# Weight pairs of a three-layer kernel: stored as pairs, and their low parts moved off GpSimd

## The chip, the cores and the metric

The kernel runs on one core of a Trainium2 chip. The time is that of the whole program on the device, in microseconds (us). TensorE (PE in the rows) multiplies matrices, VectorE (DVE) and ScalarE (ACT) do the elementwise work, GpSimd (POOL) can do some of it too, and SyncE (SP) issues most of the DMA transfers; GpSimd issues some from a queue of its own.

## What is computed

Three layers, each on the output of the one before it, all in float32:

```python
scores = where(causal, -1e9, q @ k.T / 8)                 # B, H, S, D = 4, 8, 576, 64
local  = softmax(scores) @ v
mem    = (phi(q) @ M_prev) / (phi(q) @ z_prev + 1e-6)     # phi(x) = elu(x) + 1
x      = g * mem + (1 - g) * local                        # g = sigmoid(beta); 2304 tokens x 512
h = x @ moe_w_in;   x = (s * relu(h)**2 + b) @ moe_w_out  # first layer: 512 -> 2048 -> 512
h = x @ moe2_w_in;  x = (h * tanh(softplus(h))) @ moe2_w_out   # second layer, same sizes
```

## The kernel before

**Pairs.** TensorE takes its operands in a format shorter than float32 (`F32R`). Each float32 operand is therefore held as a pair: the high part is a cast by ScalarE, the low part is the difference between the operand and its high part. A product is then three matmuls: high by high, high by low, low by high. The function `split` (L710) makes a pair; its argument `lo_on` says which engine makes the difference, and the helper line L717 records all of these differences, on either engine. L716 is the cast.

**First layer.** Its weights stay in SBUF as pairs (`wih`, `wil` for w_in, `woh`, `wol` for w_out, in four quarters `r`). The first 1536 tokens go through them in plain products (L823 and L902): four blocks of 256 tokens and one of 512.

**Block stages.** The last 768 tokens of the first layer are block 0, and the second layer is blocks 1 to 3 of 768 tokens. These use a scheme with seven products in place of eight (Winograd's form of Strassen): the operands are quarters of the matrices and sums of them. For the weights these are three quarters as they are and four sums: in w_in A00, A01, A11 and S0 to S3, in w_out B00, B10, B11 and T1 to T4. Each block has a hidden stage, eight steps `q` of seven products (L1040; the elementwise work of a step is in `hidden`, L1024), and an output stage, seven products `p` over all eight `q` (L1117, in block 0 L1120; evacuations L1108 to L1155 are in `out_product` and `out_block`).

**Where block weights come from.** For layer 1, `resident` (L773) puts the parts together again on GpSimd (L780), forms the sums, and stores all seven slots as float32 in DRAM (L790, arrays `WID[1]`, `WOD[1]`). For layer 2, `convert` (L665) turns the raw input words into float32, and `combine_in` and `combine_out` (L735, L754) form the sums on VectorE (L731) and store seven slots (L725, `WID[2]`, `WOD[2]`). `load_wi` and `load_wo` (L998, L1015) load slots back as float32 into staging tiles (`wf`, in the stage area) and split them into tiles of the ring `W`, which has four places; a hidden step and an output product each use two. GpSimd makes the differences for both w_in and w_out in block 0 and for w_out in every later block; VectorE makes those for w_in in blocks 1 to 3. In block 1 the pair of the first four w_in slots is also stored as it is (`WIS`), and blocks 2 and 3 load it with one 1 MB transfer from GpSimd's queue (L1003). `load_y` (L961) makes the 14 pairs of a block's input, with sums on L971. The 768 columns of the activations of a hidden step are, in block 0, max(x, 0) times x on VectorE (L1052) and a scale and shift on ScalarE (L1057).

**Order.** [...] A planner in the kernel file (`Plan.order`, L235) simulates all steps with estimated costs and priorities and writes out one fixed order for each engine and for SyncE's DMA queue. Buffers are rings whose places open at named points: `combined` is the end of layer 1's sums, `small_left` the end of layer 1's small blocks, `converted` the end of layer 2's conversion, and `closed` (L1259) the end of layer 1's matmuls and of `combined`; behind `closed` open the eight S places (pairs of activations for the output stage), half of the places of g2 (the activations of a hidden step), half of the PSUM banks of the block stages and the accumulators. `COMBINE` and `CONV2` are the priorities of layer 1's sums and layer 2's conversion.

Of the kernel before, what the change touches and what calls it, by code (L numbers as in the profile page):

```python
# [33 lines left out]
COMBINE = 650.0  # L34
# [25 lines left out]
def pool2_us(n):  # L60
    return 0.1 + 0.00225 * n
# [119 lines left out]
class Plan:  # L181
# [53 lines left out]
    def order(self):  # L235
# [20 lines left out]
        while True:  # L256
            e = 0
            while e < 6:
# [85 lines left out]
def attention_then_two_ffn(ctx: ExitStack, tc: tile.TileContext, qk, qz, vm, beta,  # L344
# [46 lines left out]
    WID = {x: [dram.tile([P, 2, 2, 7, P], F32, name=f"wi{x}_{r}_d") for r in range(NR)] for x in (1, 2)}  # L391
    WOD = {x: [dram.tile([P, 7, NQ2 // 2, DH], F32, name=f"wo{x}_{h}_d") for h in range(2)] for x in (1, 2)}
    WIS = [dram.tile([P, 2, 2, 4, P], F32R, name=f"wi_split{q}_d") for q in range(NQ2)]
    x_in = {(b, g): Buf() for b in range(B) for g in range(2)}
    y_in = {j: Buf() for j in range(NT // N1)}
    wi_in = {(x, r, kk): Buf() for x in (1, 2) for r in range(NR) for kk in range(2)}
    wo_in = {(x, q): Buf() for x in (1, 2) for q in range(NQ2)}
    wi_split = {}
# [336 lines left out]
    def combine_in(prio, r, kk, w0, w1):  # L735
# [12 lines left out]
        d = WID[2][r]  # L748
# [5 lines left out]
    def combine_out(prio, q, w0, w1):  # L754


        sc, landed = Buf(R["sc"], [P, 4, DH]), wo_in[2, q]

        def b_(i, j):
            return (w0, w1)[i].t.bitcast(F32)[:, j * DH:(j + 1) * DH]  # L760

        def t_(i):
            return sc.t[:, i - 1]

        sums(prio, [sc, w0, w1], [lambda: (t_(1), b_(0, 1), b_(0, 0), ALU.subtract), lambda: (t_(2), b_(1, 1), t_(1), ALU.subtract),
                                  lambda: (t_(3), b_(1, 1), b_(0, 1), ALU.subtract), lambda: (t_(4), b_(1, 0), t_(2), ALU.subtract)])
        d, x = WOD[2][q // 4], q % 4
        stored(w0, lambda: d[:, 0, x], lambda: b_(0, 0), prio, landed)
        for i in range(2):
            stored(w1, lambda i=i: d[:, 1 + i, x], lambda i=i: b_(1, i), prio, landed)  # L770
        stored(sc, lambda: d[:, 3:7, x], lambda: sc.t, prio, landed)

    def resident(prio, hi, lo, names, shape, table, bufs, landed, dest):  # L773
# [4 lines left out]
        def one(o_, x, y, op):  # L778
            def f():
                nc.gpsimd.tensor_tensor(view(made[o_].t, shape, F32), *(view(made[k].t, shape, F32) if k in made else (hi, lo)[k[0] == "l"](k[1:])  # L780
                                                                        for k in (x, y)), op=op)

            steps.append(add(POOL, pool2_us(256), prio, f, [*bufs, *(made[k] for k in {x, y} if k in made)], [made[o_]]))
# [18 lines left out]
    def resident_in(prio, r, kk):  # L802
# [3 lines left out]
        return resident(prio, lambda k: a("wih", k), lambda k: a("wil", k), ("A00", "S0", "S1", "A01", "S2", "S3", "A11"), [P, 2, P], IN_TABLE,  # L806
                        [W["wih", r], W["wil", r]], wi_in[1, r, kk], lambda x: WID[1][r][:, :, kk, x])

    def resident_out(prio, q):
# [188 lines left out]
    def load_wi(blk, q, late):  # L998

        n, x = 3 if late else 4, 2 if blk else 1  # L1000
        w, prio = Buf(R["W"], [P, 2, 2, n, P], F32R), when(blk, 0, 0, q) + 4.0 * late - 8.0
        if blk > 1 and not late:
            add(POOL, 1.0, prio, lambda: nc.gpsimd.dma_start(w.t, WIS[q]), [wi_split[q]], [w]).lag = 3.0 + load_us(16 * P)  # L1003
            return w
        wf = Buf(R["wf"], [P, 2, n, P])
        add(DMA, load_us(2 * n * P), prio, lambda: nc.sync.dma_start(wf.t, WID[x][q // 2][:, q % 2, :, 4 * late:4 * late + n]),
            [wi_in[x, q // 2, kk] for kk in range(2)], [wf])
        split(prio, (lambda x: w.t[:, x].rearrange("p a b c -> p (a b c)"), [2 * n * P], w),
              lambda: wf.t.rearrange("p a b c -> p (a b c)"), [wf], lo_on=DVE if blk else POOL)
# [5 lines left out]
    def load_wo(blk, p, half):  # L1015

        w, prio, x = Buf(R["W"], [P, 2, NQ2 // 2, DH], F32R), when(blk, 1, p, 4 * half) - 8.0, 2 if blk else 1
        slot = (0, 1, 4, 5, 3, 2, 6)[p]
        wf = Buf(R["wf"], [P, NQ2 // 2, DH])
        add(DMA, load_us(4 * DH), prio, lambda: nc.sync.dma_start(wf.t, WOD[x][half][:, slot]), [wo_in[x, 4 * half + k] for k in range(4)], [wf])  # L1020
        split(prio, (lambda x: w.t[:, x], [4, DH], w), lambda: wf.t, [wf], lo_on=POOL)
        return w

    def hidden(blk, q, prio, ew):  # L1024
# [8 lines left out]
        def product(ps, i, name, begin, end, after=()):  # L1033
            x = [y[name, 0], y[name, 1]]

            def mm():
                for part in range(3):
                    j, k = ((0, 0), (1, 0), (0, 1))[part]
                    for kk in range(2):
                        nc.tensor.matmul(ps.t[:, :H2], w[i // 4].t[:, j, kk, i % 4], x[kk].t[:, k], start=begin and part == kk == 0,  # L1040
# [8 lines left out]
        def act(at_, src, r, after=(), n=H2):  # L1049
            if blk == 0:  # L1050
                if n > H2:
                    after = [add(DVE, dve_us(n), ew, lambda: nc.vector.scalar_tensor_tensor(  # L1052
                        g.t[:, at_], src(), 0.0, src(), op0=ALU.max, op1=ALU.mult), r, [g], after)]
                else:
                    after = [add(ACT, act_us(n) + 0.06, ew, lambda: nc.scalar.activation(g.t[:, at_], src(), AF.Relu), r, [g], after)]
                    after = [add(ACT, act_us(n), ew, lambda: nc.scalar.activation(g.t[:, at_], g.t[:, at_], AF.Square), [], [g], after)]
# [142 lines left out]
    for r in range(NR):  # L1199
        for kk in range(2):  # L1200
            c1_steps["in"][r] += resident_in(COMBINE, r, kk)
    for q in range(NQ2):
        c1_steps["out"][q // 2] += resident_out(COMBINE, q)
# [4 lines left out]
    rings(m2a, opened, raw=1, yr=2, yh=2, yl=2, g=2)  # L1208
# [50 lines left out]
    closed = add(NONE, 0.0, 0.0, close_first, after=[*plan.steps[layer1:], combined])  # L1259
    low, high = Home(m1t, "low", 1024), Home(m1t, "high", 2560)  # L1260
    R["w32"] = Ring("w32b").more(m2a, 2, opened).homes(low, [0, 512], small_left).homes(high, [0, 512, 1024, 1536, 2048], small_left)
    R["sc"] = Ring("sc").more(m2a, 1, opened)
    n = len(plan.steps)
# [15 lines left out]
    raw_left = add(NONE, 0.0, 0.0, lambda: None, after=raw_steps)  # L1279

# [14 lines left out]
    R["ys2"].homes(low, [0], later).homes(high, [0, 768, 1536], later)  # L1295
    R["wf"].homes(stage, [0, 1024], raw_left).homes(stage, [2048], combined)
# [9 lines left out]
    for blk in range(NBS):  # L1306
        for q in range(NQ2):
            hidden(blk, q, 2000.0 + 20.0 * blk + q, -1000.0)
        if blk + 1 < NBS:
# [53 lines left out]
```

## Time and profile before

| | |
|---|---|
| median of 3 runs | 1045.38 us (1043.86 to 1049.28) |
| the profiled execution | 1047.22 us, of which the span from first to last instruction is 1045.5 |
| TensorE busy | 970.7 us, 93% of the span; granted clock 0.971 in the mean |
| VectorE, ScalarE, GpSimd busy | 847.1, 678.5 and 509.1 us |
| differences on GpSimd (L717) | 40 into `woh` tiles, mean 3217 ns; 32 into `wol` tiles, mean 2470 ns |
| DMA | 194.74 MB, mean 186 GB/s |

[...]

### The profile page before, as it was taken

What the parts mean: (1) busy time and instruction counts of PE and PEld (TensorE: products, weight loads), DVE (VectorE), ACT (ScalarE), POOL (GpSimd) and SP (SyncE); (2) the same over time, 40 slices, a digit from 0 to 9 for tenths busy, and PEclk for the clock granted to TensorE, in tenths of its full rate; (3) what the DMA queues carried; (4) which work ended last, traced back from release to release, by engine and by line L of the source; (5) the groups of instructions that cost most, each with busy time, mean ns of one, the idle gap of its engine ahead of it and who ended that gap; (6) DMA issues with size and microseconds to landing.
All of it is one profiled execution on the core that took longest, in us unless ns stands there. A gap on an engine that the chain in (4) does not pass through costs nothing.

```text
span 1045.5 us, 19398 instructions
## 1 busy us (share of the span) xinstructions
PE 970.7 (93%) x6600; PEld 884.7 (85%) x6600; DVE 847.1 (81%) x1716; ACT 678.5 (65%) x1415; POOL 509.1 (49%) x537
## 2 busy tenths in 40 slices
PE   6899899999999899999987879997899988999988
PEld 5577688787879899877986879997899988999988
DVE  6999998886673879888578997889777797877986
ACT  5798978888776447768776655566544565445643
POOL 5634666778775557541553351016630256401652
PEclk9999999999999999999998899999899998999989
DMA  9946757667655689968733245871656523565331
GB/s 239 286 138 186 212 163 209 178 188 202 179 159 161 198 285 309 298 234 290 261 98 110 81 161 188 290 250 58 195 185 209 196 62 117 168 234 188 101 122 61
DMA packets 126163, 194.74 MB, mean 186 GB/s; under 512 B 14448, under 2 KB 98416, under 8 KB 122992
## 3 DMA queue, kind: packets, MB, share of 16 engines
q1 hardware_dynamic: 123328, 176.72, 55.7%
q0 software_dynamic: 2304, 16.78, 4.7%
q8 instruction: 52, 0.85, 0.3%
q14 instruction: 47, 0.39, 0.1%
q10 hardware_dynamic: 432, 0.01, 0.0%
HBM read 140.51 MB, written 52.95 MB: 185 GB/s over the span
## 4 chain that ended last, share of the span: by engine, by line
PE 37%; DVE 7%; issue 4%; POOL 4%; DMA 3%; ACT 3%; SPq 0%; DVEq 0%; POOLq 0%; ACTq 0%
PE bank L1040 19%; PE bank L1117 13%; PE bank L1120 5%; POOL woh L717 3%; DVE S L717 3%; DVE wi L717 1%; DMA wo_d<-stage 1%; PE bank L902 1%; POOL wol L717 1%; DVE woh L1082 1%; DMA woh<-x_d 1%; DMA stage<-wi_d 1%; DVE wol L1082 0%; DMA raw<-in_w_out 0%; DMA stage<-in_w_out 0%
## 5 line engine op out<-in xcount | busy, mean ns | idle before, releaser
L717 POOL TENSOR_TENSOR woh<-stage,woh 128x1024 fp32r<-128x1024 f32 x40 | 128.6, 3217 | 155.0 <-ACT woh L716 90.0
L1117 PE MATMUL bank<-woh,S 128*128 128x256 f32 x864 | 122.1, 291 | 12.4 <-POOL woh L717 10.1
L1040 PE MATMUL bank<-wi,woh 128*128 128x384 f32 x546 | 125.1, 337 | 2.2 <-ACT g L874 1.8
L1117 PEld LDWEIGHTS bank<-woh,S 128*128 128x128 f32 x864 | 114.3, 199 | 14.7 <-POOL woh L717 10.5
L717 POOL TENSOR_TENSOR wol<-stage,wol 128x1024 fp32r<-128x1024 f32 (+1 forms) x32 | 79.0, 2470 | 97.0 <-ACT wol L716 96.0
L1040 PE MATMUL bank<-wi,wol 128*128 128x384 f32 x414 | 99.7, 340 | 11.0 <-DVE g L1046 6.8
L1040 PEld LDWEIGHTS bank<-wi,woh 128*128 128x128 f32 x546 | 98.5, 190 | 3.6 <-ACT g L874 2.2
L1117 PE MATMUL bank<-wol,S 128*128 128x256 f32 x648 | 90.9, 290 | 4.5 <-DVE S L717 2.6
L1117 PEld LDWEIGHTS bank<-wol,S 128*128 128x128 f32 x648 | 85.0, 198 | 5.2 <-DVE S L717 2.9
L566 ACT ACTIVATE Pt<-Pt,mx 128x64 f32<-128x64 f32 (+4 forms) x152 | 83.2, 558 | 7.9 <-DVE mx L558 7.6
L1040 PEld LDWEIGHTS bank<-wi,wol 128*128 128x128 f32 x414 | 74.5, 190 | 13.7 <-DVE g L1046 8.4
L569 POOL TENSOR_SCALAR Pt<-ex,nm 128x64 f32<-128x64 f32 x152 | 61.2, 425 | 42.6 <-DVE nm L518 24.7
L612 ACT COPY PT<-bank 128x384 f32<-128x384 f32 (+2 forms) x160 | 68.3, 489 | 18.8 <-PE bank L607 16.1
L558 DVE CUSTOM_DVE_ANT_0 Pt<-bank,mask 128x64 f32<-128x64 f32 (+3 forms) x152 | 50.1, 371 | 25.0 <-PE bank L548 16.1
L716 ACT CAST wol<-stage 128x768 fp32r<-128x768 f32 (+1 forms) x57 | 52.9, 927 | 26.3 <-PE bank L1040 23.3
L607 PE MATMUL bank<-ident,Pt 128*128 128x128 f32 x444 | 62.5, 276 | 7.5 <-DVE Pt L584 5.3
L716 ACT CAST woh<-stage 128x1024 fp32r<-128x1024 f32 x47 | 49.3, 1048 | 23.1 <-PE bank L1040 12.7
L607 PEld LDWEIGHTS bank<-ident,Pt 128*128 128x128 f32 x444 | 50.1, 141 | 11.0 <-POOL stage L687 2.7
L1040 PE MATMUL bank<-wil,wol 128*128 128x384 f32 x171 | 53.0, 349 | 2.6 <-DVE g L1046 2.6
L1003 POOL DMA_DIRECT2D woh<-wi_split_d x14 | 7.5, 534 | 93.9 <-PE bank L1040 60.5
L1120 PE MATMUL bank<-S,woh 128*128 128x384 f32 x192 | 43.3, 370 | 9.3 <-DVE S L717 8.5
L823 PE MATMUL bank<-xh,wi 128*128 128x256 f32 x256 | 44.0, 300 | 7.3 <-DVE rt L880 5.7
(321 smaller groups left out, 2711.7 us busy)
## 6 DMA issues: line engine op xcount, KB each, us to landing
stage<-wo_d SPq DMA_DIRECT2D x56, 512.0 KB, 3.5
woh<-wi_split_d POOLq DMA_DIRECT2D x14, 1024.0 KB, 5.1
stage<-wi_d SPq DMA_DIRECT2D x32, 384.0 KB, 4.3
stage<-in_w_in SPq DMA_DIRECT2D x21, 512.0 KB, 5.4
stage<-in_w_out SPq DMA_DIRECT2D x19, 512.0 KB, 4.9
stage<-wi_d SPq DMA_DIRECT2D x16, 512.0 KB, 5.0
wi_d<-stage SPq DMA_DIRECT2D x56, 128.0 KB, 2.8
wo_d<-stage SPq DMA_DIRECT2D x56, 128.0 KB, 4.7
```

The lines of the kernel that those rows point to most:

```text
L558: nc.vector.tensor_tensor_reduce(at_t(i, t, D + lo, D + hi), x.t[:, a:a + hi - lo], mask[:, SP - w + lo:SP - w + hi], -SCALE, mx.t[:, i, t ...
L566: nc.scalar.activation(at_t(i, t, D, w + D), at_t(i, t, D, w + D), AF.Exp, bias=mx.t[:, i, t + k:t + k + 1], scale=-1.0, accum_out=rs.t[:, ...
L569: add(POOL, 0.33, lambda i=i, t=t: nc.gpsimd.tensor_scalar(at_t(i, t, 0, D), ex.t[:, i, t - lo_t, :], nm.t[:, i, t - lo_t:t - lo_t + 1], 1 ...
L607: nc.tensor.transpose(ps.t[:, x, :], at_t(i, t, c * P, (c + 1) * P), ident)
L612: (nc.vector.tensor_copy if dve else nc.scalar.copy)(PT[i].t[:, x:x + n], ps.t[:, :n])
L716: hi = add(ACT, act_us(n), prio, lambda: nc.scalar.copy(t[0](0), src()), r, [t[2], half], after)
L717: lo = add(lo_on, dve_us(n) if lo_on == DVE else pool2_us(n), prio, lambda: (nc.vector if lo_on == DVE else nc.gpsimd).tensor_tensor(t[0]( ...
L823: nc.tensor.matmul(ph, w_at(nm, r, cc)[:, o:o + P], x_at(x, cc), start=(begin and part == 0 and cc == 0), stop=(part == 2 and cc == NCC - ...
L902: nc.tensor.matmul(acc[ec // per].t[:, (ec % per) * n:(ec % per + 1) * n], w_at(nm, fc // FPR, fc % FPR)[:, ec * P:(ec + 1) * P], t(x)[:, ...
L1040: nc.tensor.matmul(ps.t[:, :H2], w[i // 4].t[:, j, kk, i % 4], x[kk].t[:, k], start=begin and part == kk == 0, stop=part == 2 and kk == 1, ...
L1117: nc.tensor.matmul(acc[t].t[:, :DH], s.t[:, j, t * P:(t + 1) * P], x.t[:, k, q % 4], start=q == part == 0, stop=q == NQ2 - 1 and part == 2)
L1120: nc.tensor.matmul(acc[t].t[:, :H2], x.t[:, k, q % 4, t * P:(t + 1) * P], s.t[:, j], start=q == part == 0, stop=q == NQ2 - 1 and part == 2)
```

## The change

The high and low parts of the three plain slots of layer 1 are copied by DMA from the resident weights to DRAM (`keep_resident`, arrays `WIR`, `WOR`) and loaded back as pairs; only the four sums still go through GpSimd and are stored as float32 (`WIC`, `WOC`). Four of the seven slots of layer 2's output weights (slots 1, 2, 5, 6) are split once, when the sums are formed, and stored as pairs (`WOS`); every block loads these with a 1 MB transfer from GpSimd's queue into `W`, as block 0 does with its slots 0 to 2. What is still split at loading has its difference on VectorE. In block 0 the 768 columns of activations go to ScalarE whole (Relu, Square, scale and shift). The rings change with it: five places `sp` for the new pairs, fewer for the float32 words of layer 2 (`w32b`), one `yr` in place of two, staging tiles `wf0` of their own for block 0's w_in, and `closed` also waits for `converted`. The planner's estimate for a GpSimd operation changes, its model of the DMA queue holds issues back while more than 4 us of transfers are queued, and `COMBINE` goes from 650 to 499.

```diff
-COMBINE = 650.0
+BACKLOG = 4.0
+COMBINE = 499.0
+E_SUMS = 'PP'
...
-    return 0.1 + 0.00225 * n
+    return 0.08 + 0.0028 * n
...
-                    end, got.done = now + 0.45, dma + 1.6 + got.lag
+                    end, got.done = max(now + 0.45, dma - BACKLOG), dma + 1.6 + got.lag
...
-    def split(prio, t, src, r, after=(), lo_on=DVE):
+    def split(prio, t, src, r, after=(), done=()):
...
-        lo = add(lo_on, dve_us(n) if lo_on == DVE else pool2_us(n), prio, lambda: (nc.vector if lo_on == DVE else nc.gpsimd).tensor_tensor(
-            t[0](1), src(), t[0](0).bitcast(F32), op=ALU.subtract), [*r, half], [t[2]], after)
+        lo = add(DVE, dve_us(n), prio, lambda: nc.vector.tensor_tensor(t[0](1), src(), t[0](0).bitcast(F32), op=ALU.subtract),
+                 [*r, half], [t[2]], after)
...
-        stored(sc, lambda: d[:, 3:7, x], lambda: sc.t, prio, landed)
+        stored(w0, lambda: WOD[q // 4][:, 0, x], lambda: b_(0, 0), prio, landed)
+        stored(sc, lambda: WOD[q // 4][:, 1:3, x], lambda: sc.t[:, :2], prio, landed)
+        for slot, src, buf in ((0, lambda: b_(0, 0), w0), (1, lambda: b_(1, 0), w1), (2, lambda: b_(1, 1), w1),
+                               *((2 + i, lambda i=i: t_(i), sc) for i in range(1, 5))):
+            if slot in (0, 3, 4):
+                continue
+            y = Buf(R["sp"], [P, 2, DH], F32R)
+            split(prio, (lambda x, y=y: y.t[:, x], [DH], y), src, [buf])
+            add(DMA, load_us(2 * DH), prio, lambda y=y, slot=slot: nc.sync.dma_start(
+                d[:, slot, :, x].bitcast(F32), y.t.bitcast(F32)), [y], [landed]).lag = 1.5
...
+    def keep_resident(prio, which, r):
...
+            for slot, (i, j) in enumerate(((0, 0), (0, 1), (1, 1)) if which == "in" else ((0, 0), (1, 0), (1, 1))):
+                for o in range(2 if which == "in" else 1):
+                    def go(x=x, slot=slot, i=i, j=j, o=o, src=src):
+                        if which == "in":
+                            nc.sync.dma_start(WIR[r][:, o, x, :, slot].bitcast(F32), src(i, j)[:, o])
+                        else:
+                            nc.sync.dma_start(WOR[r // 2][:, slot, x, 2 * (r % 2):2 * (r % 2) + 2].bitcast(F32), src(i, j))
...
+        if blk == 0:
+            sums_, kept, first = (slice(0, 2), slice(2, 3), 2) if late else (slice(2, 4), slice(0, 2), 0)
+            wf = Buf(R["wf0"], [P, 2, 2, P])
+            add(DMA, load_us(4 * P), prio, lambda: nc.sync.dma_start(wf.t, WIC[q // 2][:, q % 2, :, 2 * late:2 * late + 2]),
...
+            add(DMA, load_us(4 * m * P), prio, lambda: nc.sync.dma_start(
+                w.t[:, :, :, kept].rearrange("p x k m n -> p (x k) m n").bitcast(F32),
+                WIR[q // 2][:, q % 2, :, :, first:first + m].rearrange("p x k m n -> p (x k) m n").bitcast(F32)), [wi_kept[q // 2]], [w])
+            wf0_steps.extend(split(prio, (lambda x: w.t[:, x, :, sums_], [4 * P], w), lambda: wf.t, [wf]))
...
-        split(prio, (lambda x: w.t[:, x], [4, DH], w), lambda: wf.t, [wf], lo_on=POOL)
+        if blk == 0 and slot < 3:
+            add(POOL, 1.0, prio, lambda: nc.gpsimd.dma_start(w.t, WOR[half][:, slot]), [wo_kept[half]], [w]).lag = 3.0 + load_us(8 * DH)
+        elif blk == 0 or slot in (0, 3, 4):
+            wf = Buf(R["wf"], [P, NQ2 // 2, DH])
+            add(DMA, load_us(4 * DH), prio, lambda: nc.sync.dma_start(wf.t, WOD[half][:, (0, 3, 4).index(slot)] if blk else WOC[half][:, slot - 3]), need, [wf])
+            split(prio, (lambda x: w.t[:, x], [4, DH], w), lambda: wf.t, [wf])
+        else:
+            add(POOL, 1.0, prio, lambda: nc.gpsimd.dma_start(w.t, WOS[half][:, slot]), need, [w]).lag = 3.0 + load_us(8 * DH)
...
-                if n > H2:
-                    after = [add(DVE, dve_us(n), ew, lambda: nc.vector.scalar_tensor_tensor(
-                        g.t[:, at_], src(), 0.0, src(), op0=ALU.max, op1=ALU.mult), r, [g], after)]
...
-    closed = add(NONE, 0.0, 0.0, close_first, after=[*plan.steps[layer1:], combined])
+    closed = add(NONE, 0.0, 0.0, close_first, after=[*layer1_steps, combined, converted])
```

## Rows read from the trace of the kernel before

**Rows 1.** Chain that ended last, by time: start us, us, what.

```profile
493.11 1.59 PE bank L1040 x6
...
644.55 1.04 PE bank L1040 x6
...
777.83 1.04 PE bank L1040 x6
...
786.28 50.63 PE bank L1040 x292
...
852.75 14.46 POOL woh L717
...
893.87 16.82 PE bank L1117 x138
...
910.69 1.04 PE bank L1040 x6
...
1002.30 40.02 PE bank L1117 x318
```

**Rows 2.** Windows by stage: stretch, us, busy us of each engine, clock, DMA share, GB/s.

```profile
493.00:573.00 80.00, 69.47 (x357) 65.93 (x358) 59.23 (x86) 57.72 (x97) 39.28 (x17) 0.93 0.51 163
573.00:644.50 71.50, 60.67 (x307) 58.91 (x307) 67.17 (x93) 41.57 (x75) 30.73 (x11) 0.88 0.34 113
...
705.00:777.80 72.80, 63.47 (x487) 62.15 (x488) 64.89 (x106) 41.97 (x79) 42.40 (x13) 0.95 0.44 136
...
837.00:910.70 73.70, 65.11 (x489) 63.54 (x488) 64.80 (x108) 42.48 (x79) 42.75 (x13) 0.93 0.38 113
...
970.00:1045.50 75.50, 67.30 (x523) 65.91 (x522) 61.42 (x88) 38.11 (x67) 34.45 (x12) 0.95 0.29 91
```

**Rows 3.** Waits of TensorE, 493 to 645 and 645 to 780: us, times, longest.

```profile
PE bank L1120 <- DVE S L717: 10.0, 4, 4.5
...
PE bank L1117 <- POOL woh L717: 5.0, 1, 5.0
```

**Rows 4.** Timelines of three engines where block 2 turns to its output stage.

```profile
839.19 2.44 POOL L717 TENSOR_TENSOR woh<-stage,woh 128x1024 fp32r<-128x1024 f32 x1 [2.52 <-ACT woh L716]
...
839.34 2.70 DVE L717 TENSOR_TENSOR wi<-high,wi 128x384 fp32r<-128x384 f32 x1
...
842.57 2.29 PE L1040 MATMUL bank<-wil,wol 128*128 128x384 f32 x6 [2.61 <-DVE g L1046]
...
848.98 0.55 DVE L971 TENSOR_TENSOR low<-high,low 128x384 f32<-128x384 f32 x1
849.45 0.55 DVE L1108 TENSOR_TENSOR woh<-woh 128x384 f32<-128x384 f32 x1
```

**Rows 5.** Windows of line 717 alone: VectorE and GpSimd busy us, clock, DMA, GB/s.

```profile
573.00:644.50 71.50, 53.88 (x63) 30.73 (x11) 0.88 0.34 113
705.00:777.80 72.80, 48.49 (x63) 41.62 (x12) 0.95 0.44 136
837.00:910.70 73.70, 45.65 (x63) 42.18 (x12) 0.93 0.38 113
970.00:1045.50 75.50, 42.68 (x49) 34.45 (x12) 0.95 0.29 91
```

**Rows 6.** Groups of instructions by shape: count, busy us, mean ns, idle before them.

```profile
L716 ACT CAST woh<-stage 128x1024 fp32r<-128x1024 f32 x47 | 49.3, 1048 | 23.1 <-PE bank L1040 12.7 <-issue 5.3 <-DMA stage<-wi_d 2.6
...
L717 DVE TENSOR_TENSOR woh<-stage,woh 128x1024 fp32r<-128x1024 f32 x7 | 8.5, 1215 | 0.0
```

**Rows 7.** Line 1003: issue ns min, median, max; then us to landing.

```profile
L1003 POOL DMA_DIRECT2D wol<-wi_split_d x2: 567/670/774, 769.8 to 902.6; - x2
...
DMA to landing us min/median/max: 5.0/5.2/7.1
```

**Rows 8.** Last conversions of layer 2: line 731's first and last start, last store.

```profile
L731 DVE TENSOR_TENSOR sc<-low x3: 418/424/951, 442.3 to 494.6; 128x256 f32<-128x256 f32 x3
...
496.19 0.37 SPq L725 DMA_DIRECT2D wo_d<-sc  x1
```

More of the change, by code (lines that the diff above doesn't have):

```diff
@@ L397, in attention_then_two_ffn @@
     wo_in = {(x, q): Buf() for x in (1, 2) for q in range(NQ2)}
+    wi_kept, wo_kept = {r: Buf() for r in range(NR)}, {h: Buf() for h in range(2)}
     wi_split = {}
@@ L998, in load_wi @@
     def load_wi(blk, q, late):
-        n, x = 3 if late else 4, 2 if blk else 1
+        n = 3 if late else 4
         w, prio = Buf(R["W"], [P, 2, 2, n, P], F32R), when(blk, 0, 0, q) + 4.0 * late - 8.0
@@ L1015, in load_wo @@
     def load_wo(blk, p, half):
[L1017 to L1020, printed above, removed]
-        split(prio, (lambda x: w.t[:, x], [4, DH], w), lambda: wf.t, [wf], lo_on=POOL)
+        w, prio = Buf(R["W"], [P, 2, NQ2 // 2, DH], F32R), when(blk, 1, p, 4 * half) - 8.0
+        slot, need = (0, 1, 4, 5, 3, 2, 6)[p], [wo_in[2 if blk else 1, 4 * half + x] for x in range(4)]
+        if blk == 0 and slot < 3:
[6 more added lines that the diff above has]
+            add(POOL, 1.0, prio, lambda: nc.gpsimd.dma_start(w.t, WOS[half][:, slot]), need, [w]).lag = 3.0 + load_us(8 * DH)
         return w
@@ L1034, in product @@
             x = [y[name, 0], y[name, 1]]
+            at_ = (0, 2, 3, 1)[i] if blk == 0 and i < 4 else i % 4
             def mm():
@@ L1039, in mm @@
                     for kk in range(2):
-                        nc.tensor.matmul(ps.t[:, :H2], w[i // 4].t[:, j, kk, i % 4], x[kk].t[:, k], start=begin and part == kk == 0,
+                        nc.tensor.matmul(ps.t[:, :H2], w[i // 4].t[:, j, kk, at_], x[kk].t[:, k], start=begin and part == kk == 0,
                                          stop=part == 2 and kk == 1, skip_group_check=not begin)
@@ L1199, in attention_then_two_ffn @@
     for r in range(NR):
+        for which in ("in", "out"):
+            c1_steps[which][r] += keep_resident(COMBINE, which, r)
         for kk in range(2):
-            c1_steps["in"][r] += resident_in(COMBINE, r, kk)
+            c1_steps["in"][r] += resident_in(on(E_SUMS[kk]), COMBINE, r, kk)
     for q in range(NQ2):
-        c1_steps["out"][q // 2] += resident_out(COMBINE, q)
+        c1_steps["out"][q // 2] += resident_out(on(E_SUMS[q % 2]), COMBINE, q)
     combined = add(NONE, 0.0, 0.0, lambda: None, after=[x for y in c1_steps.values() for z in y.values() for x in z])
@@ L1207, in attention_then_two_ffn @@
     R["h"].banks(banks[1:2], opened)
-    rings(m2a, opened, raw=1, yr=2, yh=2, yl=2, g=2)
+    rings(m2a, opened, raw=1, yr=1, yh=2, yl=2, g=2)
     for i in range(4):
@@ L1294, in attention_then_two_ffn @@
         R["W"].homes(Home(wpool, nm, 2048, F32R), [0], after)
-    R["ys2"].homes(low, [0], later).homes(high, [0, 768, 1536], later)
-    R["wf"].homes(stage, [0, 1024], raw_left).homes(stage, [2048], combined)
+    R["ys2"].homes(low, [0], later).homes(Home(m1t, "high", 2560), [0, 768, 1536], later)
+    R["wf"].homes(stage, [0, 1024], raw_left)
+    R["wf0"], wf0_steps = Ring("wf0").homes(stage, [2048, 2560], combined), []
     for nm, after in (("wih3_0", left[3]), ("wil3_0", left[3]), ("woh2_0", out_left[2]), ("wol2_0", out_left[2]),
@@ L1308, in attention_then_two_ffn @@
             hidden(blk, q, 2000.0 + 20.0 * blk + q, -1000.0)
+        if blk == 0:
+            R["wf"].homes(stage, [2048], add(NONE, 0.0, 0.0, lambda: None, after=[converted, *wf0_steps]))
         if blk + 1 < NBS:
```

64 lines of the change are left out of this document (40 added, 24 removed).

## Prediction

> **What bounds the kernel now.** I read the windows by stage first, then the chain that ended last, then what TensorE waited for, then the timeline of one turn from a hidden stage to an output stage. Up to about 493 us TensorE is all but full; what can still be won lies behind it. The chain dates the stages [rows 1]: block 0 runs from 493.11 to 644.55, block 1 to 777.83, block 2 to 910.69, block 3 to the end of the span at 1045.5 (all in us). [...]
>
> A floor for each block comes from its undisturbed stretches [rows 1]: 292 hidden matmuls take 50.63, 0.1734 each; 138 output matmuls take 16.82, 0.1219 each. A hidden stage is 8 x 7 x 6 = 336 matmuls, 58.3; an output stage of blocks 1 to 3 is 504, 61.4; that of block 0 is 336 of the wide kind, 58.3. So blocks 1 to 3 could take 119.7 and take 133.3, 132.9 and 134.8 (of the last, 3.1 is the tail behind the last matmul). Block 0 also carries 32 layer-1 matmuls of 512 columns (0.231 each by the 0.1734 of 384 columns, together 7.4): floor 124.0, taken 151.4. Lost: 27.4 + 13.6 + 13.2 + 12.0 = 66.2, idle time and low clock together.
>
> What sits in those gaps is one quarrel between two engines. TensorE waits for VectorE's S pieces in block 0, 10.0 in all, and for GpSimd's weight difference once in each of blocks 1 and 2, 5.0 a time [rows 3]. The timeline of block 2 [rows 4] shows why. A GpSimd difference starts at 839.19 and a VectorE difference of 384 columns at 839.34: VectorE's takes 2.70, though the same operation starts every 0.47 elsewhere, and TensorE then idles 2.61 for the next VectorE result. The other way round, from 848.98 on VectorE starts a new one every 0.47, and a GpSimd difference that begins at 852.75 takes 14.46 [rows 1]; one of the 5.0 waits of TensorE stands behind it. Each makes the other wait for whole instructions.
>
> [...]
>
> **The change, part by part.**
> *GpSimd's 72 differences go* (16 and 14 in block 0, 14 in each later block). They fill 42.18 of GpSimd's 42.75 in block 2's output stage [rows 2, 5]. What VectorE gets back there: its 63 differences of line 717 take 45.65 [rows 5]; at 0.47 each they would take 29.6, so 16.0 is waiting. By the same working, 18.9 in block 1, 19.7 in block 3 (49 of them). In block 0, seven of the 63 are of 1024 columns (1.215 each [rows 6]), so 8.5 + 56 x 0.47 = 34.8 in place of 53.88: 19.1.
>
> *What VectorE takes over.* In each of blocks 1 to 3 six weight tiles of 1024 columns, 6 x 1.215 = 7.3; in block 0's output stage eight, 9.7; in block 0's hidden stage sixteen of 512 columns, at half price 9.7, against eight squares of 768 columns that leave it for ScalarE (by the same 1.215, 0.91 each, 7.3). VectorE's load afterwards: block 0 out 67.2 - 19.1 + 9.7 = 57.8 against a floor of 58.3; block 1 out 64.9 - 18.9 + 7.3 = 53.3 against 61.4; block 2 out 56.1; block 3 out 49.0. It fits, tightly in block 0.
>
> *Direct loads.* Slots 1, 2, 5 and 6 of blocks 1 to 3 and slots 0 to 2 of block 0 come as 1 MB pairs by GpSimd's queue straight into W; 24 + 6 casts of 1.048 [rows 6] leave ScalarE, which is not the bound there. Loads of exactly this size and queue exist: issue 0.57 to 0.77, landing 5.0 to 7.1 [rows 7]. W has four tiles; an output product uses two, 4.4 each (504 x 0.1219 / 14), so a tile has 3 x 4.4 = 13.2 to be refilled and needs at most 0.8 + 7.1 = 7.9. Cost nothing, hidden by the three other tiles; cover 5.3; without it each load would cost TensorE its own lateness.
>
> *ScalarE in block 0's hidden stage.* It gains Relu and Square on 768 columns, loses casts of 1024 and 768 and gains two of 512, for each of 8 q. By 1.048 per 1024 columns that is +1.57 - 1.83 + 1.05 = +0.8 a piece, 6.3. The window's 57.72 becomes 64.0, against a TensorE floor of 65.7 (58.3 + 7.4). ScalarE nearly becomes the bound there, so I keep half of that stretch's loss.
>
> *Stores and their queues.* 48 stores of sums go (112 to 64), 72 of resident parts come, which wait for no arithmetic and can go as soon as the weights are converted; layer 2's output weights bring 32 casts and 32 differences of 256 columns and larger stores. The sync queue issues 40 more stores; block 0's hidden stage has 16 more loads there and the output stages 30 fewer. The stores lie beside a TensorE that is all but full; I take 0, with 4 either way, since the new order also moves GpSimd's sums, which stay on GpSimd and go on blocking VectorE ahead of block 0. The stores and `closed` are a rival below.
>
> *The sum.* Not all loss goes. Hidden stage of block 0: lost 80.0 - 65.7 = 14.3, half kept, gain 7. Its output stage: lost 13.2, VectorE full, 6 kept, gain 7. Blocks 1 and 2: VectorE at 87 and 91%, so one wait of the 2.6 kind and a short stretch at 1.2 GHz are kept, 4 each: gains 9.6 and 9.2. Block 3: 3 kept, gain 9.0. Together 41.8 from the profiled execution's 1047.2: 1005.4. That execution was 1.8 above the median of the runs, so I state 1004. If nothing is kept the gain is 66.2 and the time 979.
>
> **The rivals.**
> *VectorE and ScalarE stay the bound (half gain).* For it: 57.8 of 58.3 in block 0 and a VectorE that must also wait for ScalarE's halves and TensorE's banks. Against it: the load has slack in three of four blocks. If half of the 41.8 is kept, 1024.
>
> *The 1 MB loads come late.* For it: the load can start only when its W tile is free, whereas the staged 512 KB were fetched ahead. Against it: cover 5.3. It eats the whole gain when each of 30 loads is 1.4 late beyond the cover, about 14.6 from issue to use. A GpSimd issue that is held like the 14.46 difference would do this once a block. Four such at 14.5 - 5.3 = 9.2 give 37 back: 1041. Two issues that now fall in full VectorE work took 0.57 and 0.77 [rows 7], against it. [...]
>
> *Slower: `closed` comes late.* S, half of g2 and four PSUM banks of the block stages now open only when all layer-2 weights are stored. The output weights' combining now runs from 442.3 to the store at 496.19 [rows 8]; layer 1 frees the banks at about 511. The new splits pass through five `sp` buffers: 32/5 rounds of cast (0.3), difference (0.4) and store (5.0 to 7.1, by the landings at hand) are 37 to 50, so 479 to 492 by that bound, and 4.2 MB more to store, at 5.0 to 7.1 for each MB, adds 21 to 30: 500 to 522 at the latest. Block 0 needs the first of it for its fifth q, at 493 + 7.4 + 4 x 7.3 = 530. So no cost by rows; but if stores that wait in the one sync queue hold up loads behind them, it grows one for one, and from `closed` at 572 on the change is a loss. At 585 it costs 55: 1059.
>
> *The new order gives back early what is won late.* Every queue is ordered anew by other estimated costs; the stretch ahead of 493, where TensorE is all but full, would have to lose 42: 1045.
>
> **How the numbers follow.** Forecast, all blocks gain as summed, 979 to 1017: 0.62. Half gain, 1017 to 1036: 0.21. Late loads, 1036 to 1048: 0.05, half of it within 0.5%. Late `closed`, slower: 0.09. Order: 0.03, within 0.5%. Runs of this kernel differ by 5 us, so 0.5% is what a measurement can tell. Faster 0.86, same 0.05, slower 0.09. Range 980 to 1036: it holds the first two cases, some 0.82.
>
> **What would show it.** Right: line 717 gone from GpSimd; 384-column VectorE differences at 0.55 everywhere behind 500; block starts about 123 apart in place of 133; no TensorE wait on GpSimd; a clock of 0.97 or more in the output stages. Wrong: TensorE waits on W loads at the second product of an output stage (late loads); on VectorE S pieces throughout (half gain); a hole in block 0 at its fifth q (`closed`); or VectorE differences still at 1.2 and more with GpSimd idle, in which case the quarrel was not the cause.

## The result and the profile after

The changed kernel takes 979.2 us (median of 4 runs, 976.9 to 981.1) against 1046.6 for the kernel before: ratio 0.9355, 95% interval 0.9322 to 0.9389. The forecast was 1004 with a range of 980 to 1036. The direction and the place were right; the gain is 67 where 42 was forecast, 0.8 us outside the range.

The chain that ended last dates the stages again (start, us, what):

```profile
507.06 0.93 PE bank L939 x4
...
558.18 55.35 PE bank L1170 x318
613.53 1.04 PE bank L1094 x6
...
731.44 1.31 PE bank L1094 x6
...
850.38 1.13 PE bank L1094 x6
...
913.00 60.48 PE bank L1167 x504
```

L1094, L1167, L1170 and L725 are now what L1040, L1117, L1120 and L717 were. Against [rows 1], blocks 1 to 3 take 977.0 - 613.5 = 363.5 where they took 401.0: 37.5 won. Blocks 1 and 2 are 117.9 and 118.9 long, where the prediction looked for about 123. Their start has moved from 644.55 to 613.53; layer 1's last matmuls (L939) start at 507.06 where those of before started at 509.78, so 2.7 comes from ahead of that point and 28.3 from the rest of block 0. Together 68.5, the whole difference of the two spans. Output matmuls stand at 0.120 each for a whole stage (60.48 / 504), a little under the 0.1219 that the floor was worked out from.

Windows by stage, the columns as in [rows 2] (TensorE, its weight loads, VectorE, ScalarE, GpSimd, clock, DMA share, GB/s); the second fence is line 725 alone, VectorE only:

```profile
493.00:556.00 63.00, 62.05 (x341) 59.03 (x340) 50.89 (x102) 58.22 (x107) 1.83 (x3) 1.00 0.84 281
556.00:613.40 57.40, 57.40 (x331) 56.95 (x330) 57.03 (x108) 43.94 (x83) 1.58 (x3) 1.00 0.56 176
...
672.00:731.40 59.40, 59.03 (x485) 58.82 (x483) 51.12 (x105) 35.38 (x70) 4.83 (x10) 1.00 0.70 238
...
790.00:850.20 60.20, 60.20 (x493) 60.18 (x492) 52.43 (x108) 36.98 (x73) 4.75 (x9) 1.00 0.63 208
913.00:977.00 64.00, 60.47 (x505) 60.26 (x503) 42.49 (x85) 29.60 (x57) 3.70 (x7) 1.00 0.47 158
```

```profile
790.00:850.20 60.20, 37.11 (x67) 1.00 0.63 208
```

The second row is the one to look at. In block 0's output stage VectorE is busy 57.03 of 57.40 us, and TensorE 57.40 of 57.40. The granted clock, as a share of full speed, is 1.00 in each of these stretches, where [rows 2] had 0.88 to 0.95. Line 725 does 67 operations in 37.11 us, four of them of 1024 columns; in [rows 5] 63, all of 384 columns, took 45.65.

What TensorE waited for behind 500 us, all of it (us, times, longest), against the 10.0 and 5.0 of [rows 3]:

```profile
PE bank L1094 <- ACT wol L1112: 0.6, 1, 0.6
PE bank L1094 <- DMA woh<-wi_split_d: 0.4, 1, 0.4
PE bank L1094 <- ACT g L1112: 0.2, 1, 0.2
```

The turn of block 2 to its output stage, VectorE's timeline, which answers to [rows 4]: a start every 0.47, no 2.70 in it, and a 1024-column difference between them at 1.23.

```profile
799.57 0.56 DVE L725 TENSOR_TENSOR S<-wil,S 128x384 fp32r<-128x384 f32 x1
800.04 1.23 DVE L725 TENSOR_TENSOR wol<-stage,wol 128x1024 fp32r<-128x1024 f32 x1
801.18 0.56 DVE L1158 TENSOR_TENSOR wil<-wil 128x384 f32<-128x384 f32 x1
801.64 0.56 DVE L725 TENSOR_TENSOR S<-woh,S 128x384 fp32r<-128x384 f32 x1
```

### The profile page after: what moved, and what is told of

Read it like the earlier page. It is cut to its first block, busy times and chain, and to the rows that moved or that the text cites. A ratio compares the mean times of both kernels' runs of the same rounds, so it can differ in the third digit from the quotient of the medians.

```text
span 977.0 us, 19335 instructions
## 1 busy us (share of the span) xinstructions
PE 944.4 (97%) x6599; PEld 865.5 (89%) x6599; DVE 799.1 (82%) x1782; ACT 666.0 (68%) x1433; POOL 312.5 (32%) x495
## 4 chain that ended last, share of the span: by engine, by line
PE 45%; issue 7%; DVE 6%; ACT 6%; DMA 5%; POOL 1%; SPq 0%; POOLq 0%; DVEq 0%; ACTq 0%
PE bank L1094 18%; PE bank L1167 13%; PE bank L1170 6%; PE bank L939 3%; PE bank L860 3%; DMA wo_sums_d<-stage 1%; DVE sc L739 1%; DVE stage L701 1%; DMA woh<-wi_split_d 1%; DMA wi_d<-sc 1%; DVE w32b L703 1%; PE bank L637 1%; DMA woh<-x_d 1%; DVE gl L922 1%; PE bank L615 1%
## 5 line engine op out<-in xcount | busy, mean ns | idle before, releaser
L1094 PE MATMUL bank<-wi,woh 128*128 128x384 f32 x546 | 118.5, 336 | 1.3 <-ACT wol L1112 0.6
L1167 PE MATMUL bank<-wol,S 128*128 128x256 f32 x792 | 107.3, 283 | 0.0
L1167 PEld LDWEIGHTS bank<-wol,S 128*128 128x128 f32 x792 | 101.0, 192 | 0.0
L1094 PEld LDWEIGHTS bank<-wi,woh 128*128 128x128 f32 x546 | 96.2, 188 | 3.2 <-ACT wol L1112 0.9
L1167 PE MATMUL bank<-woh,S 128*128 128x256 f32 x720 | 97.4, 283 | 0.0
L1094 PE MATMUL bank<-wi,wol 128*128 128x384 f32 x414 | 96.1, 335 | 0.0
L1167 PEld LDWEIGHTS bank<-woh,S 128*128 128x128 f32 x720 | 91.4, 192 | 0.0
L1094 PEld LDWEIGHTS bank<-wi,wol 128*128 128x128 f32 x414 | 73.9, 188 | 0.9 <-DVE woh L1100 0.6
L1074 POOL DMA_DIRECT2D woh<-wo_split_d x13 | 6.9, 528 | 164.1 <-DVE g L1100 76.2
L725 DVE TENSOR_TENSOR woh<-stage,woh 128x1024 fp32r<-128x1024 f32 (+2 forms) x38 | 39.0, 1027 | 9.6 <-ACT woh L724 9.5
L724 ACT CAST woh<-stage 128x1024 fp32r<-128x1024 f32 (+2 forms) x38 | 33.8, 889 | 18.4 <-PE bank L1094 15.6
L724 ACT CAST S<-g 128x384 fp32r<-128x384 f32 x56 | 28.8, 513 | 24.6 <-PE bank L1167 19.2
L917 DVE SCALAR_TENSOR_TENSOR rt<-bank,rt 128x512 f32<-128x512 f32 x32 | 22.0, 686 | 24.8 <-ACT rt L911 24.7
L592 POOL TENSOR_SCALAR Pt<-Pt,rs 128x64 f32<-128x64 f32 (+2 forms) x72 | 38.6, 557 | 10.4 <-DVE rs L595 6.5
```

Source lines behind the costliest of these rows:

```text
L592: (nc.vector if e == DVE else nc.gpsimd).tensor_scalar(x, x, r, *((None, ALU.mult) if e == DVE else (1.0, ALU.mult, ALU.mult)))
L725: lo = add(DVE, dve_us(n), prio, lambda: nc.vector.tensor_tensor(t[0](1), src(), t[0](0).bitcast(F32), op=ALU.subtract), [*r, half], [t[2] ...
L1094: nc.tensor.matmul(ps.t[:, :H2], w[i // 4].t[:, j, kk, at_], x[kk].t[:, k], start=begin and part == kk == 0, stop=part == 2 and kk == 1, s ...
L1167: nc.tensor.matmul(acc[t].t[:, :DH], s.t[:, j, t * P:(t + 1) * P], x.t[:, k, q % 4], start=q == part == 0, stop=q == NQ2 - 1 and part == 2)
```

## The experiments

Each run is compared with the kernel before on the same chip; ratios stand with their 95% interval. Two theories stood against each other. Q: GpSimd's and VectorE's two-input operations block one another, and that is the loss. L: the stored pairs win by taking work away from ScalarE and VectorE.

**One part alone, on the kernel before.** All 72 differences on VectorE; no stored pairs.

```diff
-              lambda: wf.t.rearrange("p a b c -> p (a b c)"), [wf], lo_on=DVE if blk else POOL)
+              lambda: wf.t.rearrange("p a b c -> p (a b c)"), [wf])
...
-        split(prio, (lambda x: w.t[:, x], [4, DH], w), lambda: wf.t, [wf], lo_on=POOL)
+        split(prio, (lambda x: w.t[:, x], [4, DH], w), lambda: wf.t, [wf])
```

> The kernel before with one edit: all 72 weight differences of the block stages on VectorE, none on GpSimd; no stored pairs, no direct loads. Theory Q (the quarrel: GpSimd's differences and VectorE's two-input operations block one another for whole instructions, and that is the loss behind 493 us): VectorE's output-stage load in block 2 goes from 64.8 to 64.8 - 16.0 + 14 x 1.215 = 65.8 against a floor of 61.4, so a little loss stays; block starts 124 to 127 apart in place of 133, total about 1010 (1000 to 1020), 384-column VectorE differences at 0.55. Theory L (the load: what won is the work that stored pairs take away, 30 casts on ScalarE and as many differences): VectorE only gets fuller, total 1040 or more.

Measured: 983.9, ratio 0.9396 (0.9348 to 0.9445). Two arguments of a function bring 62 of the 67 us, and the interval overlaps that of the kernel after, so the other 5 cannot be told from nothing. L falls: VectorE got all 72 differences and the kernel is faster. Q holds, and beats its own forecast by 26 us. The order of every queue was planned anew in this run, so it doesn't yet say how much is the engine and how much the order. The windows of the output stages of blocks 0 and 2 show why (columns as above):

```profile
560.00:619.90 59.90, 56.27 (x316) 55.63 (x315) 59.75 (x111) 42.56 (x78) 0.00 (x0) 0.98 0.46 139
...
795.00:855.40 60.40, 60.40 (x494) 60.40 (x493) 59.71 (x116) 44.23 (x82) 0.53 (x1) 1.00 0.47 138
```

In block 2 VectorE is busy 59.71 of 60.40 and TensorE does not idle at all. Only in block 0, at 59.75 of 59.90, does TensorE lose 3.6.

**That part undone, on the kernel after.** The 42 differences still made at loading go back to GpSimd.

```diff
-        lo = add(DVE, dve_us(n), prio, lambda: nc.vector.tensor_tensor(t[0](1), src(), t[0](0).bitcast(F32), op=ALU.subtract),
+        lo = add(lo_on, dve_us(n) if lo_on == DVE else pool2_us(n), prio, lambda: (nc.vector if lo_on == DVE else nc.gpsimd).tensor_tensor(t[0](1), src(), t[0](0).bitcast(F32), op=ALU.subtract),
...
-            wf0_steps.extend(split(prio, (lambda x: w.t[:, x, :, sums_], [4 * P], w), lambda: wf.t, [wf]))
+            wf0_steps.extend(split(prio, (lambda x: w.t[:, x, :, sums_], [4 * P], w), lambda: wf.t, [wf], lo_on=POOL))
...
-            split(prio, (lambda x: w.t[:, x], [4, DH], w), lambda: wf.t, [wf])
+            split(prio, (lambda x: w.t[:, x], [4, DH], w), lambda: wf.t, [wf], lo_on=POOL)
```

> The kernel after with one edit: the 42 weight differences that are still made at loading (16 and 8 in block 0, 6 in each of blocks 1 to 3) go back to GpSimd; stored pairs and direct loads stay. Theory Q: the loss comes back by the share of differences, 6/14 of some 39 in blocks 1 to 3 and 24/30 of some 27 in block 0, about 38: 1005 to 1020, VectorE differences over 1 us beside GpSimd's. Theory L: GpSimd is idle there and takes 42 operations off a VectorE that is at 80 to 100%: 975 to 985.

Measured: 1005.3, ratio 0.9605 (0.9557 to 0.9653), 26 us lost again, at the low end of what Q gave. TensorE waits for GpSimd as it did before, so this run alone doesn't tell blocking from weights that come late:

```profile
PE bank L1167 <- POOL wol L725: 6.8, 2, 3.4
...
PE bank L1170 <- POOL woh L725: 5.7, 1, 5.7
```

**GpSimd work that nobody waits for.** Behind each direct load of blocks 1 to 3, operations on the attention's mask, which nothing uses any more: four subtractions of 320 columns; in a second run eight fills, `nc.gpsimd.memset(x, 0.0)`, in their place.

```diff
+    def idle():
+        x = mask.bitcast(F32)
+        for _ in range(4):
+            nc.gpsimd.tensor_tensor(x, x, x, op=ALU.subtract)
...
-            add(POOL, 1.0, prio, lambda: nc.gpsimd.dma_start(w.t, WOS[half][:, slot]), need, [w]).lag = 3.0 + load_us(8 * DH)
+            add(POOL, 1.0, prio, lambda: [nc.gpsimd.dma_start(w.t, WOS[half][:, slot]), idle()], need, [w]).lag = 3.0 + load_us(8 * DH)
```

> The kernel after, and behind each of the 24 direct output-weight loads of blocks 1 to 3 GpSimd does four subtractions of 320 columns on a tile that nothing uses any more (the mask of the attention; the output doesn't change). Nobody waits for them. Theory Q: they block VectorE and are blocked by it; 24 x 4 x 0.8 = 77 us of GpSimd work that reads SBUF, VectorE differences beside them at 1 us and more, VectorE full in the output stages, TensorE waits for S: 985 to 1005. If only GpSimd's lateness mattered (weights that TensorE waits for), 979 as before the edit.

> As the run with subtractions, but with eight fills of 320 columns, which write and read nothing. If the blocking is over GpSimd's reading of SBUF, VectorE's differences stay at 0.55 and the time at 979. If any GpSimd work beside VectorE blocks it, the time goes up as with the subtractions.

Measured: 1000.8 with subtractions (0.9565, 0.9521 to 0.9608), 981.9 with fills (0.9378, 0.9332 to 0.9424). Groups by shape behind block 0 (count, busy us, mean ns), first with subtractions, then with fills:

```profile
L725 DVE TENSOR_TENSOR S<-woh,S 128x384 fp32r<-128x384 f32 x42 | 31.2, 743 | 0.1
...
L1201 DVE TENSOR_TENSOR xh<-bank,xh 128x256 f32<-128x256 f32 x27 | 9.9, 412 | 0.0
...
L1066 POOL TENSOR_TENSOR mask<-mask 128x320 f32<-128x320 f32 x96 | 108.4, 1129 | 6.2
```

```profile
L725 DVE TENSOR_TENSOR S<-woh,S 128x384 fp32r<-128x384 f32 x42 | 23.3, 554 | 3.9 <-ACT S L724 3.9
...
L1201 DVE TENSOR_TENSOR xh<-bank,xh 128x256 f32<-128x256 f32 x27 | 10.0, 418 | 0.0
...
L1066 POOL MEMSET mask<- 128x320 f32 x192 | 70.7, 368 | 9.7
```

In the run with 71 us of fills VectorE's differences keep their 554 ns; in the run with 108 us of subtractions they take 743. That mean mixes two kinds. Of the 196 differences of 384 columns behind block 0, the 102 that overlap a subtraction in time take 894 in the mean, the 94 that overlap none 548; with fills the two means are 555 and 554. The sums with one input from PSUM are the control. Those of the evacuations (L1201, 256 columns) take 411 beside a subtraction (27 of them) and 416 apart from one.

So what the two runs show is a quarrel over reading SBUF: VectorE's operations with both inputs in SBUF take 894 beside GpSimd operations that read it and 555 beside those that only write it, and its sums with one input from PSUM keep their time beside the former (411). Behind block 0 TensorE waits 12.8 us with subtractions: 7.4 for VectorE's S, 2.6 for evacuations, 0.4 for g, 1.9 for ScalarE, and 0.5 for a w_in pair. It waits for no output-weight load, although four subtractions at 689.21 took 12.93 and held back the next one in GpSimd's queue. All 22 us are lost in the output stages of blocks 1 and 2 (68.2 and 74.0 where the kernel after has 59.4 and 60.2, at a granted clock of 0.95); block 3's, where VectorE has less to do, is as long as before the edit. Late loads do appear in the run with fills: there TensorE's only waits behind block 0 are for two w_in pairs from GpSimd's queue, 3.0 in all.

**The engine alone, the order kept.** The kernel before, planned with GpSimd's cost and place; only when the instructions are written out does a difference go to VectorE. The queues of TensorE, ScalarE and SyncE are then instruction for instruction those of before.

```diff
-        lo = add(lo_on, dve_us(n) if lo_on == DVE else pool2_us(n), prio, lambda: (nc.vector if lo_on == DVE else nc.gpsimd).tensor_tensor(
+        lo = add(lo_on, dve_us(n) if lo_on == DVE else pool2_us(n), prio, lambda: nc.vector.tensor_tensor(
```

> The kernel before, planned as it was, with GpSimd's cost and place in the plan; only when the instructions are written out does each of the 72 differences go to VectorE's queue, at the place where the plan had it start. So every other instruction keeps its order, and only the engine changes. If the blocking itself is the loss, most of the 62 us of the first run come back without a new plan: 985 to 1005. If the new plan did it (VectorE's order written for VectorE's own load), this stays at 1020 or more, since each difference holds up what stands behind it in VectorE's queue.

Measured: 1007.9, ratio 0.9646 (0.9613 to 0.9679), between the two forecasts. The engine under the old order gives 37 of the 62: the end of the blocking, and of weights that come late from GpSimd (10.9 of TensorE's waits before), which this run doesn't part. The other 25 come with the order planned anew for a VectorE that does this work. Under the old order VectorE's differences stand at 0.55 as well, and TensorE still waits for S:

```profile
701.66 0.55 DVE L717 TENSOR_TENSOR S<-g,S 128x384 fp32r<-128x384 f32 x1
...
PE bank L1117 <- DVE S L717: 10.0, 4, 3.8
```

**Parts of the changed kernel undone one at a time.** The planner's constants of before; max(x, 0) times x back on VectorE; the 30 output loads on the sync queue; layer 2's output weights as seven float32 slots (`combine_out` and `load_wo` as before, differences on VectorE).

```diff
+COMBINE = 650.0
+    return 0.1 + 0.00225 * n
+                    end, got.done = now + 0.45, dma + 1.6 + got.lag
```

> The kernel after with the three planner constants of before (no hold on the DMA queue, priority of layer 1's sums back at 650, the old estimate for GpSimd). If the quarrel theory holds, the new constants bring little: 977 to 985. If the order matters by itself (the rival that the stretch ahead of block 0 moves), block 0 starts more than 5 us later than 488 or the blocks show TensorE waits on transfers: 990 or more.

```diff
+                if n > H2:
+                    after = [add(DVE, dve_us(n), ew, lambda: nc.vector.scalar_tensor_tensor(
+                        g.t[:, at_], src(), 0.0, src(), op0=ALU.max, op1=ALU.mult), r, [g], after)]
```

> The kernel after with max(x, 0) times x on 768 columns in block 0 back on VectorE. The prediction held that ScalarE nearly becomes the bound of block 0's hidden stage and kept 7 us of loss for it. If that is so, taking some 13 us off ScalarE there shortens block 0: 974 to 977. If ScalarE has room, nothing changes: 978 to 982.

```diff
-            add(POOL, 1.0, prio, lambda: nc.gpsimd.dma_start(w.t, WOS[half][:, slot]), need, [w]).lag = 3.0 + load_us(8 * DH)
+            add(DMA, load_us(8 * DH), prio, lambda: nc.sync.dma_start(w.t.bitcast(F32), WOS[half][:, slot].bitcast(F32)), need, [w])
```

> The kernel after with the 30 direct loads of output weights on the sync queue in place of GpSimd's. If GpSimd's queue were held by VectorE's work, this is faster by some us. If the 5.3 us of cover hide either queue, 977 to 983. If loads that wait for a W tile hold up the others behind them in the one sync queue, slower: 985 to 1000.

```diff
-        elif blk == 0 or slot in (0, 3, 4):
+        else:
             wf = Buf(R["wf"], [P, NQ2 // 2, DH])
...
-        else:
-            add(POOL, 1.0, prio, lambda: nc.gpsimd.dma_start(w.t, WOS[half][:, slot]), need, [w]).lag = 3.0 + load_us(8 * DH)
```

> The kernel after without stored pairs for layer 2's output weights: seven float32 slots as before, every one cast by ScalarE and its difference made by VectorE at loading; block 0 keeps its stored pairs. VectorE in an output stage of blocks 1 to 3 gets 8 x 1.215 = 9.7 more, to about 60 of 60. If a full VectorE costs TensorE something, each block is 3 to 6 us longer: 988 to 997. If a full VectorE whose order is right costs nothing (the first run says so), 977 to 983.

| undone | us | ratio, interval |
|---|---|---|
| nothing (the kernel after) | 979.2 | 0.9355, 0.9322 to 0.9389 |
| planner's constants | 986.4 | 0.9429, 0.9401 to 0.9457 |
| max(x, 0) times x on ScalarE | 976.5 | 0.9340, 0.9314 to 0.9365 |
| output loads on GpSimd's queue | 980.1 | 0.9371, 0.9348 to 0.9394 |
| layer 2's stored pairs | 976.6 | 0.9340, 0.9316 to 0.9364 |

The last three cannot be told from no edit. For max(x, 0) times x that settles nothing: 976.5 lies inside the 974 to 977 that stood for a ScalarE near its bound, and the interval holds no edit too. The stored pairs of layer 2 are worth nothing that can be measured: without them VectorE works 60.02 us in the 60.70 of block 2's output stage, and TensorE is full. The queue of the loads makes no difference. The planner's constants are worth 7, a little more than forecast: with the old ones block 0's first hidden products lie 7 us later in the chain, from the stretch ahead. On the kernel before the same constants, beside the differences on VectorE, go the other way:

> The kernel before with all weight differences on VectorE and the three planner constants of after, nothing else. On the kernel after these constants are worth 7 us. If the quarrel and the order are all there is in the change, 976 to 980; if block 0's stored pairs are worth their 9 us beside them, 984 or more.

Measured: 991.3, ratio 0.9482 (0.9448 to 0.9516), against 983.9 without them. By its number this falls under "984 or more", but that stood for no gain; neither forecast foresaw a loss. Layer 1's last matmuls start at 516.44 in this run and at 509.76 without the constants, so the loss lies ahead of that point; its cause stays open. An order planned from estimates moves by 7 us either way. So does what the rest of the change is worth: beside the old constants nothing (986.4 with it, 983.9 without), beside the new ones some 12 (979.2 against 991.3). Block 0's stored pairs were not undone alone, and which part of the change makes that difference is not shown.

**What is left of GpSimd's two-input work.** Layer 1's 144 sums on VectorE too, on the kernel after:

```diff
-E_SUMS = 'PP'
+E_SUMS = 'DD'
```

> The kernel after with layer 1's sums (144 operations of 256 columns) on VectorE too, so that GpSimd makes no two-input operation behind the attention. VectorE gets 144 x 0.34 = 49 us between 175 and 470. If the quarrel is worth anything ahead of block 0 (VectorE differences and conversions at 1.2 in place of 0.7 beside it, TensorE idle some 7 us between 325 and 493), 970 to 977. If VectorE, at 81 to 85% of those stretches, is then the bound, TensorE waits for rt: 982 to 1000.

Measured: 967.1, ratio 0.9258 (0.9236 to 0.9281), 12 us faster than the kernel after by the medians, 10 by the ratios, and 3 below the better forecast. The stretch ahead of block 0 and one shape of its conversions on VectorE (count, busy us, mean ns), first of the kernel after, then with the edit:

```profile
325.00:493.00 168.00, 161.27 (x1010) 143.53 (x1009) 142.47 (x213) 113.17 (x210) 86.17 (x94) 1.00 0.84 265
...
L701 DVE SCALAR_TENSOR_TENSOR stage<-stage 128x512 int32<-128x512 int32 x20 | 18.6, 928 | 1.5 <-ACT stage L699 1.5
```

```profile
325.00:493.00 168.00, 168.00 (x1044) 151.99 (x1044) 141.70 (x301) 121.36 (x223) 0.00 (x0) 1.00 0.87 278
...
L701 DVE SCALAR_TENSOR_TENSOR stage<-stage 128x512 int32<-128x512 int32 x21 | 14.3, 687 | 5.4 <-ACT stage L699 5.3
```

VectorE does 301 operations in the time in which it did 213, its conversions (L701) go from 928 to 687 ns, and TensorE's 6.7 us of idle time are gone. Layer 1's last matmuls start 9.4 earlier, so nearly all of the gain lies ahead of that point. The order was planned anew here too; the two were not parted for this edit.

Two runs put the edits together: layer 2 as float32 with max(x, 0) times x on VectorE, and these two with the sums on VectorE. A third is the kernel before with all 72 differences and all 144 sums on VectorE, and nothing else.

> The kernel after without layer 2's stored pairs and with max(x, 0) times x on VectorE in block 0: the two edits that alone came out at 976.5 against 979.2. If both gains are real and add up, 973 to 975; if they are scatter, 976 to 980.

> The kernel after with layer 1's sums on VectorE, layer 2's output weights as float32 and max(x, 0) times x on VectorE: the three edits that were worth 12, 2.6 and 2.7 alone. If they add, 962 to 965. If VectorE, which gets all three, is now the bound, 967 or more.

> The kernel before with every two-input operation that GpSimd had behind the attention on VectorE (72 differences and 144 sums), no stored pairs, no direct output loads, the old planner constants. If the quarrel is the whole cause and stored pairs are worth little, 966 to 974. If the pairs, which take 56 of VectorE's differences away, are what lets a full VectorE keep up in block 0, 978 to 985.

Measured: 972.2 (0.9312, 0.9283 to 0.9341); 964.9 (0.9234, 0.9195 to 0.9273); 970.1 (0.9281, 0.9247 to 0.9315). The first is below the kernel after by 7 in the medians and by 4.5 in the ratios, whose intervals overlap, so that gain is not shown; the second is the fastest run and can't be told from the one with the sums alone. The third beats the changed kernel without any stored pair or new load: engine choices, with the order planned for them, are worth 74 us on the kernel before. It can't be told from the kernel after with the sums on VectorE (0.9258), so beside these choices the rest of the change is worth nothing that can be measured.

## Why the prediction was right and wrong

*What bounds the kernel: right.* The quarrel was named as the cause of the gaps, with its place and its two directions, and the floors were right: 119.7 a block by the rows, 118.7 by the full stages after (336 hidden matmuls at the 54.08 / 312 of block 3, and 60.48). The runs show the cause: the engine changed with the order kept brings 37, and GpSimd reads that nobody waits for cost 22 where fills cost nothing that can be measured. But it was named as the one cause, and it is not all of the loss: some 25 us stay when it ends under the old order.

*The step that failed is the sum's "Not all loss goes".* It kept 24 of the 66 us because VectorE and ScalarE would be nearly full: 7 in block 0's hidden stage for ScalarE, 6 in its output stage, 4, 4 and 3 later. Measured, next to nothing is kept: block 0 wins 28.3 where 14 was forecast and 27.4 was lost, blocks 1 to 3 win 37.5 where 27.8 was forecast and 38.8 was lost. The short stretch at 1.2 GHz that the sum kept in blocks 1 and 2 is a term that no run shows: the traces have no clock in GHz. They show a granted clock of 0.50 from 867 to 871 before, behind one of the 5.0 waits, and of 1.00 in the output stages of both blocks after. A nearly full VectorE did not cost TensorE what was kept for it; the runs with VectorE at 59.71 of 60.40 and 60.02 of 60.70, TensorE without a gap, show it. What the order has to do with it is shown less directly. Under the old order VectorE has room (49.86 of the 60.00 us from 700 to 760), and TensorE still waits 10.0 for S; a queue planned for the load brings 25 more. That points at the place in VectorE's queue of the pieces that TensorE needs next. That the old order's gain of 37 lies near the 41.8 of the forecast is a coincidence: the sum kept its 24 for full engines, and gave the planning anew no term.

*VectorE's load in block 0's output stage: right by luck.* The sum took seven of the 63 differences there to be of 1024 columns. Only one is; the seven of [rows 6] are counted over the whole trace. With one, the time that VectorE gets back is 23.5 in place of 19.1 and its load 53.4 in place of 57.8. Measured are 57.03 of 57.40, but in a stretch that holds 108 operations, where the 93 of before and the eight added make 101.

*ScalarE near its bound: the load about right, the loss not.* The forecast had 64.0 of ScalarE's work in a stretch of 65.7. The stretch that answers to it begins, as that one did, with layer 1's last 32 matmuls still to come, and ends with the first output product:

```profile
492.10:558.20 66.10, 65.15 (x358) 61.96 (x358) 53.13 (x106) 61.31 (x114) 1.83 (x3) 1.00 0.85 279
```

ScalarE is busy 61.31 of 66.10, and the stretch is 0.4 over its floor where 7 was kept. The run with max(x, 0) times x on VectorE doesn't decide whether even that is ScalarE's.

*The 14.46: read as a wait for whole instructions, but longer than any.* The prediction says that each engine makes the other wait for whole instructions. The 2.70 of VectorE agrees: it ends 0.4 behind GpSimd's difference. The 14.46 does not: no instruction of VectorE beside it takes more than 0.56. From 852.75 on VectorE starts some 25 more two-input operations, the last of them

```profile
864.45 0.55 DVE L717 TENSOR_TENSOR wi<-high,wi 128x384 fp32r<-128x384 f32 x1
```

and then stands idle. GpSimd ends at 867.21, 2.2 behind that one, about its time alone (2.35 at best). So it was kept out for the whole run of operations and not for one. The four subtractions at 689.21, which took 12.93, show the same: they come through when VectorE turns to sums with one input from PSUM at 698.69.

*Ahead of block 0: taken as 0 with 4 either way, measured 2.7.* That was right in size, but it stopped the argument too soon. The prediction itself says that GpSimd's sums go on blocking VectorE there; taking them off GpSimd was worth 10 to 12.

*The direct loads: right, cost nothing.* TensorE waited for none of them; its one wait for a DMA behind 500, 0.4, is for a w_in pair (`wi_split_d`). The issues beside VectorE's work stayed at 0.53, for all 24 of the stored pairs (ns, min, median, max):

```profile
L1074 POOL DMA_DIRECT2D woh<-wo_split_d x13: 527/527/530, 672.1 to 959.7; - x13
L1074 POOL DMA_DIRECT2D wol<-wo_split_d x11: 527/528/532, 676.3 to 952.2; - x11
```

Behind 660, where these loads are, VectorE does nothing but `tensor_tensor`, so these rows say nothing of an issue beside its other operations.

*`closed`: right, no cost.* The store of the last pair was issued at 508.8; with 3.3 to 8.9 to landing that is 512 to 518, inside the 500 to 522 worked out, and no hole stands at block 0's fifth q:

```profile
L784 SPq DMA_DIRECT2D wo_split_d<-high x32: 359/433/982, 435.2 to 508.8; - x32
...
DMA to landing us min/median/max: 3.3/4.7/8.9
```

*The range* ended at the time with nothing kept, 979 rounded to 980, and left no room for a gain ahead of block 0. That the 979 of "nothing is kept" is the measured time to the microsecond is luck in part: 65.8 of the 66.2 came back behind layer 1, and 2.7 ahead of it. A floor worked out from rows is a case of its own and should have had a chance of its own.

## What to carry to other kernels

When two engines stand in each other's way, try the engine of the operation before anything that saves operations: two arguments gave 62 us, the machinery of stored pairs nothing more that could be told, and putting the rest of GpSimd's two-input work on an already busy VectorE 10 to 12 again. Read the mean of one shape beside and apart from the other engine's work; a share of busy time hides it, since waiting for the other engine counts as busy (the difference of 14.46, 2.35 at best, stands as 14.46 of GpSimd's work). And an engine near 100% need not be a loss by itself (VectorE at 59.71 of 60.40, TensorE without idle time): ask what stands ahead of the critical pieces in its queue.

## What the runs showed of the hardware

GpSimd fills (320 columns) run beside VectorE's operations with two SBUF inputs without a trace: 369 ns beside them and 366 apart, and VectorE's 384 columns take 555 and 554. GpSimd subtractions of the same size take 720 apart and 1152 beside in the mean, and VectorE's 384 columns 894 beside them and 548 apart. VectorE's operations with one input from PSUM (256 columns) take 411 beside subtractions and 416 apart. A difference of 1024 columns takes VectorE 1.22 us; on GpSimd it took 2.35 at best and, begun beside a run of some 25 VectorE operations without gaps, 14.46: it was not let in between them, and ended 2.2 behind the last.
